# Moving the query maxima and one rounding between engines in an attention and MoE kernel

## The chip, the cores and the metric

The kernel runs on one core of a Trainium2 chip. The metric is the device time of one execution in microseconds. Five engines work side by side, each through its own list of instructions in order: TensorE (PE in the profile, its weight loads PEld), VectorE (DVE), ScalarE (ACT), GpSimd (POOL), and SyncE (SP), which issues the transfers. They wait for each other by semaphores.

## The reference

Attention with a feature map in place of the softmax, and then a two-layer network over its output. Everything is float32.

```python
def phi(x):
    proj = np.einsum('bhsd,df->bhsf', x, w_phi)
    proj = proj - np.max(np.abs(proj), axis=-1, keepdims=True)
    return np.concatenate([np.exp(proj), np.exp(-proj)], axis=-1)
q_p, k_p = (phi(q), phi(k))                     # 8 batches, 8 heads, 576 tokens, 64 -> 256
kv = np.einsum('bhsf,bhsd->bhfd', k_p, v)
z = np.sum(k_p, axis=2)
num = np.einsum('bhsf,bhfd->bhsd', q_p, kv)
den = np.einsum('bhsf,bhf->bhs', q_p, z)[..., None] + 1e-06
x = (num / den)                                 # laid out as 4608 tokens x 512
h = x @ w_in                                    # 512 -> 2048
g = np.maximum(0.01 * h, h)
out = g @ w_out                                 # 2048 -> 512
```

The maximum of the absolute projection is taken per token and head over 128 features. It is what the change is about.

## The kernel before

Two heads form an item; there are 8 batches of 4 items, 32 in all. For an item i, `k_phase(i)` makes the feature map of the keys and from it `kv` and `z`, and the query phase makes the feature map of the queries, multiplies it by them and divides. The results go into `ring`, which holds two batches of attention output. Items 0 to 7 take other forms of these phases (`first_k_phase`, `first_q_phase`, `token_q_phase`, and the `nat` branch of `k_phase`); the change does not touch them. Items 8 to 31 use `q_phase` and the other branch of `k_phase`.

Matrix products are made of float32 values that are split in two: `xh` is the value rounded to the format in which TensorE multiplies at its full rate (`F32R`), and `xl` the rest. Each product is then three: high by high, high by low, low by high. A rounding is a cast (`copy_`, line 67 on ACT, line 69 on VectorE), and the rest a subtraction (`tt_`, line 72, on POOL or VectorE). The table `ENG` says which engine does which: `"qh": "v"` puts the rounding of the query exponentials on VectorE, `"kpl": "pppv"` three of four key subtractions on POOL, and what has no entry, `"ql"` and `"gl"` among it, goes to POOL for subtractions and to ACT for copies.

`q_phase` works in a layout with features on the 128 partitions and tokens along them. For each of the two heads j and each half u of the 576 tokens, two matmuls give the projection, and a VectorE transpose of 32x32 blocks (line 380) puts it into `tq`. Line 382 takes the largest absolute value of each block row: `m` then holds, for each head, 18 values on each partition. As the transposes go block by block, the 128 features of a token are still spread over four groups of 32 partitions, and the maximum has to be taken across these groups, and given back to all four. Lines 384 to 389 do that with six small VectorE instructions: copy the upper 64 partitions next to the lower ones, take the larger of the two, the same for 32 partitions, and copy the result back to the other 32, and then to the other 64.

Then for each head, line 396 subtracts the maximum, line 398 transposes back into `mb`, and for each half lines 403 and 404 take the two exponentials on ACT into `eq`; `copy_("qh", ...)` rounds them and `tt_("ql", ...)` makes the rest. Lines 415, 416 and 418 multiply by the keys' sums, lines 420 and 421 bring numerator and denominator out of PSUM, and 424 to 429 divide. Of two buffers each are `eq` and `ql`; `qh` holds both halves of a head.

The MoE layers go by blocks of 256 tokens and 16 steps of 128 hidden features. `layer1` gives `h` in PSUM (lines 615, 616, 618); ACT makes `g` (line 622) and rounds it to `gh`, POOL subtracts to `gl`; `layer2` (lines 635 to 637) runs three steps later (`LAG`). `g`, `gh` and `gl` have two buffers each, and so has `h`. `split` rounds the attention output of the next block to `xh` and `xl`.

Nothing is ordered by hand on the engines. A scheduler places every instruction by priority, by when its inputs and buffers come free, and by durations that it assumes; attention has the better priority (`PA`) over the MoE. `advance` lets the attention run ahead, up to two batches. So what stands in an engine's list is settled before the run, and a change of engine or operation in one place moves the order everywhere behind it.

Of the kernel before, what the change touches and what calls it, by code (L numbers as in the profile page):

```python
# [9 lines left out]
F32 = mybir.dt.float32  # L10
# [4 lines left out]
ALU = mybir.AluOpType  # L15
AX = mybir.AxisListType

P = 128
# [13 lines left out]
NK = 8  # L32
BUFS = {"kph": 2, "eq": 2, "m4": 2, "g": 2, "gh": 2, "gl": 2, "ql": 2}
PBUFS = {"a": 3, "c": 1, "h": 2, "acc": 2}
ENG = {"vh": "a", "kst": "v", "qh": "v", "o": "av", "kl": "pv", "kpl": "pppv", "ksub": "vvp", "l": "v"}
TINY = 2.0 ** -15
HUGE = 2.0 ** 16 * 1.875
PF = -10 ** 6
# [6 lines left out]
def attention_moe_kernel(ctx: ExitStack, tc: tile.TileContext, q, k, v, vt, w_phi, w_in, w_out, out):  # L45
    nc = tc.nc
# [4 lines left out]
    def ct(shape, dt, name):  # L51
        return cp.tile(shape, dt, tag=name, name=name)

    def st(shape, dt, tag):
        return sp.tile(shape, dt, tag=tag, name=tag, bufs=BUFS.get(tag, 1))
# [3 lines left out]
    def pick(key):  # L59
        n = cnt[key] = cnt.get(key, -1) + 1  # L60
        e = ENG.get(key, "")
        return e[n % len(e)] if e else None

    def copy_(key, o, i):
        e = pick(key) or "a"
        if e == "a":
            nc.scalar.copy(o, i)  # L67
        else:
            (nc.vector if e == "v" else nc.gpsimd).tensor_copy(o, i)  # L69

    def tt_(key, o, a, b, op):
        (nc.vector if pick(key) == "v" else nc.gpsimd).tensor_tensor(o, a, b, op=op)  # L72

    def pt(tag):
        return ps.tile([P, 512], F32, tag=tag, name=tag, bufs=PBUFS[tag])
# [20 lines left out]
    vh = ct([P, 10, 66], F32R, "vh")  # L96
# [44 lines left out]
    for j in range(2):  # L141
        r = slice(64 * j, 64 * j + 64)
        c = slice(F * j, F * j + F)
# [39 lines left out]
    def load_q(i):  # L183
        rq = st([P, S], F32, "rq")
        nc.sync.dma_start(rq, q[i])
        qraw[i] = rq
# [112 lines left out]
    def blocks(x):  # L299
        return x.rearrange("p a b -> p (a b)").rearrange("p (c d) -> p c d", d=32)  # L300
# [60 lines left out]
    def q_phase(i):  # L361
        b, hp = divmod(i, NP)
        rq = qraw.pop(i)
        qs = st([P, 2, S], F32R, "qs")
        for j in range(2):
            o, n = slice(64 * j, 64 * j + 64), slice(64 - 64 * j, 128 - 64 * j)
            copy_("qx", qs[o, j], rq[o])
            nc.vector.tensor_tensor(qs[n, j], rq[o], qs[o, j].bitcast(F32), op=ALU.subtract)  # L368
        if i + 1 < B * NP:
            load_q(i + 1)  # L370
        yield
        tq = st([P, 2, 2, U], F32, "tq")
        m = st([P, 2, 18], F32, "m")
        for j in range(2):
            for u in range(2):
                pq = pt("a")[:, 0:U]
                rs = qs[:, j, U * u : U * u + U]
                nc.tensor.matmul(pq, lhsT=wq_h, rhs=rs, start=True, stop=False)
                nc.tensor.matmul(pq, lhsT=wq_l, rhs=rs, start=False, stop=True)
                nc.vector.transpose(tq[:, j, u], pq)  # L380
                yield
            nc.vector.tensor_reduce(m[:, j], blocks(tq[:, j]), axis=AX.X, op=ALU.max, apply_absolute_value=True)
        ms = st([64, 2, 18], F32, "ms")
        nc.vector.tensor_copy(ms, m[64:128])
        nc.vector.tensor_tensor(m[0:64], m[0:64], ms, op=ALU.max)
        nc.vector.tensor_copy(ms[0:32], m[32:64])
        nc.vector.tensor_tensor(m[0:32], m[0:32], ms[0:32], op=ALU.max)
        nc.vector.tensor_copy(m[32:64], m[0:32])
        nc.vector.tensor_copy(m[64:128], m[0:64])
        yield  # L390
        kvh, kvl = kvs_of[i]
        dn = tq[:, 0]
        qhs = st([P, 2, 2, U], F32R, "qh")
        for j in range(2):
            tj = blocks(tq[:, j])
            nc.vector.tensor_tensor(tj, tj, m[:, j].unsqueeze(2).broadcast_to([P, 18, 32]), op=ALU.subtract)  # L396
            mb = st([P, 2, U], F32, "mb")
            nc.vector.transpose(mb.rearrange("p a b -> p (a b)"), tq[:, j].rearrange("p a b -> p (a b)"))  # L398
            yield
            es = []  # L400
            for u in range(2):
                eq = st([P, 2, U], F32, "eq")
                nc.scalar.activation(eq[:, 0], mb[:, u], AF.Exp)  # L403
                nc.scalar.activation(eq[:, 1], mb[:, u], AF.Exp, scale=-1.0)  # L404
                qh = qhs[:, u]
                ql = st([P, 2, U], F32R, "ql")
                copy_("qh", qh, eq)
                tt_("ql", ql, eq, qh.bitcast(F32), ALU.subtract)
                es.append((qh, ql))
                yield  # L410
            for u in range(2):
                qh, ql = es[u]
                nm = pt("a")[:, 0:U]
                for t in range(2):
                    nc.tensor.matmul(nm, lhsT=kvh[:, j, t], rhs=qh[:, t], start=t == 0, stop=False)
                    nc.tensor.matmul(nm, lhsT=kvl[:, j, t], rhs=qh[:, t], start=False, stop=False)
                for t in range(2):
                    nc.tensor.matmul(nm, lhsT=kvh[:, j, t], rhs=ql[:, t], start=False, stop=t == 1)
                rr = slice(64 * j, 64 * j + 64)
                nc.scalar.copy(ring[rr, b % 2, hp, U * u : U * u + U], nm[0:64])  # L420
                nc.scalar.activation(dn[rr, u], nm[64:128], AF.Copy, bias=1e-6)
                yield
        dt = st([P, 2, U], F32, "mb")
        nc.vector.transpose(dt.rearrange("p a b -> p (a b)"), dn.rearrange("p a b -> p (a b)"))
        rc = st([P, 18], F32, "rc")
        nc.vector.reciprocal(rc, blocks(dt)[:, :, 0])
        nc.vector.transpose(blocks(dt), rc.unsqueeze(2).broadcast_to([P, 18, 32]))
        x = ring[:, b % 2, hp]
        tt_("x", x, x, dt.rearrange("p a b -> p (a b)"), ALU.mult)
        yield  # L430
# [153 lines left out]
    def attention():  # L584
        for i in range(NP, B * NP + 1):
            gens = [k_phase(i)] if i < B * NP else []
            if i > NP:
                gens.append((token_q_phase if i - 1 < NN else q_phase)(i - 1))
            while gens:
                for it in list(gens):  # L590
                    if next(it, end) is end:
                        gens.remove(it)
                    else:
                        yield i - 1
            yield i
# [126 lines left out]
```

## Time and profile before

| | |
|---|---|
| median of 3 runs | 1253.36 us (1252.39 to 1255.06) |
| the profiled execution | 1253.03 us, span 1251.2 us |
| PE busy | 1184.7 us, 95% of the span |
| DVE busy | 840.5 us, 67% |
| ACT busy | 804.3 us, 64% |
| POOL busy | 691.0 us, 55% |
| granted TensorE clock | 0.993 |

The span is the time from the first to the last instruction of the profiled execution; its own time is 1.8 us longer. Engines are busy while an instruction of theirs executes. Matmuls overlap in TensorE's pipeline, so that one that is listed with 284 ns may start 120 ns after the one before it. In a group's row stand line, engine, operation, output and inputs by name, shapes, count, then busy time in us and mean ns of one, then the idle time just before them and what ended it. The row of a wait says who waited for whom, us in total, times, and the longest. The first 190 us hold the loads, the weights' preparation and the first eight items; the items of the kind that the change touches follow up to about 1077 us, mixed with MoE work; the rest is MoE alone.

### The profile page before, as it was taken

To read this page: it belongs to the slowest core of one execution; us is meant where nothing else is said; L and a number is where in the kernel's file an instruction comes from. 1 tells how busy PE (TensorE), PEld (TensorE's weight loads), DVE (VectorE), ACT (ScalarE), POOL (GpSimd) and SP (SyncE) were. 2 spreads that over 40 slices of the span, in tenths; PEclk is the share of its full clock that TensorE was granted. 3 is DMA by queue.
4 is the path that set the end of the run, shared out by engine and by line. 5 is a ranking of instruction groups with operands and counts; after the bars stand their busy time and mean duration, and the time that the engine had idled before them with its cause. 6 is when DMAs were issued, how large, how long until landed. Compare 5 with 4: busy or idle time off the path is not lost. (4 is left out here: it accounts for less than half of the span.)

```text
span 1251.2 us, 21516 instructions
## 1 busy us (share of the span) xinstructions
PE 1184.7 (95%) x7654; PEld 1045.7 (84%) x7654; DVE 840.5 (67%) x1349; ACT 804.3 (64%) x2048; POOL 691.0 (55%) x724
## 2 busy tenths in 40 slices
PE   6889899999998999899999999999999999999998
PEld 5577688898887888788898888899997889999997
DVE  7999843478788877788888788854888887300000
ACT  6897865767667776666776667764776767433232
POOL 3233232457685776666676677764676867433232
PEclk9999999999998999999999999999999999999999
DMA  6544510211111101111111111020111110000000
GB/s 189 155 125 140 141 52 13 57 31 30 47 31 47 29 29 31 30 39 29 48 30 48 31 39 39 10 58 28 30 24 37 28 38 1 18 17 1 18 17 18
DMA packets 62779, 57.02 MB, mean 46 GB/s; under 512 B 45136, under 2 KB 46288, under 8 KB 62672
## 3 DMA queue, kind: packets, MB, share of 16 engines
q1 hardware_dynamic: 62672, 55.65, 15.8%
q8 instruction: 60, 0.98, 0.3%
q14 instruction: 47, 0.39, 0.1%
HBM read 46.20 MB, written 9.44 MB: 44 GB/s over the span
## 5 line engine op out<-in xcount | busy, mean ns | idle before, releaser
L72 POOL TENSOR_TENSOR gl<-g,gh 128x256 fp32r<-128x256 f32 x288 | 242.4, 846 | 275.1 <-ACT gh L67 214.7
L615 PE MATMUL h<-xh,w0h 128*128 128x256 f32 x1152 | 295.2, 284 | 6.7 <-ACT dn L567 2.2
L616 PE MATMUL h<-xh,w0l 128*128 128x256 f32 x1152 | 293.5, 282 | 1.3 <-DVE w0l L72 1.3
L615 PEld LDWEIGHTS h<-xh,w0h 128*128 128x128 f32 x1152 | 217.9, 189 | 18.7 <-ACT dn L567 3.0
L635 PE MATMUL acc<-w1h,gh 128*128 128x512 f32 x576 | 229.5, 399 | 2.9 <-DVE o L69 1.8
L636 PE MATMUL acc<-w1l,gh 128*128 128x512 f32 x576 | 228.0, 396 | 0.0
L616 PEld LDWEIGHTS h<-xh,w0l 128*128 128x128 f32 x1152 | 218.0, 189 | 11.5 <-DVE w0l L72 2.1
L637 PE MATMUL acc<-w1h,gl 128*128 128x512 f32 x576 | 218.3, 396 | 0.2 <-POOL gl L72 0.2
L618 PE MATMUL h<-xl,w0h 128*128 128x256 f32 x1152 | 201.7, 283 | 0.7 <-POOL xl L72 0.7
L622 ACT ACTIVATE g<-h 128x256 f32<-128x256 f32 x288 | 108.1, 383 | 133.0 <-PE h L618 93.1
L72 POOL TENSOR_TENSOR ql<-eq,qh 128x576 fp32r<-128x576 f32 x96 | 153.0, 1601 | 71.8 <-DVE qh L69 59.8
L618 PEld LDWEIGHTS h<-xl,w0h 128*128 128x128 f32 x1152 | 164.7, 189 | 3.1 <-POOL xl L72 2.0
L67 ACT CAST gh<-g 128x256 fp32r<-128x256 f32 x288 | 114.8, 404 | 70.4 <-PE acc L636 68.5
L72 POOL TENSOR_TENSOR kpl<-ek,kph 128x512 fp32r<-128x512 f32 x72 | 104.3, 1449 | 34.6 <-ACT kph L67 17.3
L635 PEld LDWEIGHTS acc<-w1h,gh 128*128 128x128 f32 x576 | 108.8, 189 | 16.7 <-DVE o L69 2.7
L637 PEld LDWEIGHTS acc<-w1h,gl 128*128 128x128 f32 x576 | 105.7, 188 | 19.1 <-POOL gl L72 1.3
L636 PEld LDWEIGHTS acc<-w1l,gh 128*128 128x128 f32 x576 | 109.1, 189 | 12.8
L69 DVE CAST qh<-eq 128x576 fp32r<-128x576 f32 x96 | 95.6, 1002 | 35.7 <-ACT eq L404 24.7
L250 ACT ACTIVATE ek<-pmk 128x256 f32<-128x256 f32 (+1 forms) x128 | 53.4, 417 | 64.8 <-POOL kpl L72 27.5
L69 DVE COPY o<-acc 128x512 f32<-128x512 f32 x17 | 11.5, 677 | 124.2 <-DMA out_dram<-o 124.0
L403 ACT ACTIVATE eq<-mb 128x288 f32<-128x288 f32 x96 | 42.2, 439 | 81.6 <-DVE mb L398 77.9
L72 POOL TENSOR_TENSOR ring<-ring,mb 128x576 f32<-128x576 f32 (+2 forms) x45 | 52.1, 1158 | 66.7 <-DVE mb L573 18.3
(227 smaller groups left out, 2505.6 us busy)
## 6 DMA issues: line engine op xcount, KB each, us to landing
out_dram<-o SPq DMA_DIRECT2D x35, 256.0 KB, 2.0
rk<-in_k_dram SPq DMA_DIRECT2D x30, 288.0 KB, 2.8
ring<-in_w_in_dram SPq DMA_DIRECT2D x16, 512.0 KB, 3.6
qh<-in_w_out_dram SPq DMA_DIRECT2D x16, 512.0 KB, 3.6
rq<-in_q_dram SPq DMA_DIRECT2D x28, 288.0 KB, 2.9
rv<-in_v_dram SPq DMA_DIRECT2D x30, 256.0 KB, 3.5
rv<-in_vt_dram SPq DMA_DIRECT2D x60, 32.0 KB, 2.9
f<-in_k_dram SPq DMA_DIRECT2D x2, 288.0 KB, 4.2
```

The costliest lines, as they stand in the source:

```text
L67: nc.scalar.copy(o, i)
L69: (nc.vector if e == "v" else nc.gpsimd).tensor_copy(o, i)
L72: (nc.vector if pick(key) == "v" else nc.gpsimd).tensor_tensor(o, a, b, op=op)
L250: nc.scalar.activation(ek[r, :, 0:F], pmk[r, 2 * s : 2 * s + 2], AF.Exp)
L403: nc.scalar.activation(eq[:, 0], mb[:, u], AF.Exp)
L615: nc.tensor.matmul(ph, lhsT=weight(0, "h", ft)[:, d * P : d * P + P], rhs=xh[:, d], start=d == 0, stop=False)
L616: nc.tensor.matmul(ph, lhsT=weight(0, "l", ft)[:, d * P : d * P + P], rhs=xh[:, d], start=False, stop=False)
L618: nc.tensor.matmul(ph, lhsT=weight(0, "h", ft)[:, d * P : d * P + P], rhs=xl[:, d], start=False, stop=d == NP - 1)
L622: nc.scalar.activation(g, ph, AF.Prelu, alpha=0.01)
L635: nc.tensor.matmul(a, lhsT=gh[:, ts], rhs=weight(1, "h", ft), start=ft == 0, stop=False)
L636: nc.tensor.matmul(a, lhsT=gh[:, ts], rhs=weight(1, "l", ft), start=False, stop=False)
L637: nc.tensor.matmul(a, lhsT=gl[:, ts], rhs=weight(1, "h", ft), start=False, stop=ft == NFT - 1)
```

## The change

The rounding of the query exponentials, `qh`, goes from VectorE to ACT: one letter in `ENG`. It is 96 instructions on 128x576 values.

The six small instructions become six others. `m` is now the first half of a tile `mm` of twice the size. What were copies between partition groups are now `tensor_reduce` with the maximum over a last axis of length one, which hands each value on as it is (`one`). What were two-input maxima are `tensor_reduce` over a last axis of length two: the partner's values have been put beside one's own in the other half of the tile (`mm[:, 1]`, `ms[:, 1]`), and the pair is viewed as the last axis. The values are the same.

```diff
-ENG = {"vh": "a", "kst": "v", "qh": "v", "o": "av", "kl": "pv", "kpl": "pppv", "ksub": "vvp", "l": "v"}
+ENG = {"vh": "a", "kst": "v", "qh": "a", "o": "av", "kl": "pv", "kpl": "pppv", "ksub": "vvp", "l": "v"}
...
-        m = st([P, 2, 18], F32, "m")
+        mm = st([P, 2, 2, 18], F32, "m")
+        m = mm[:, 0]
...
-        ms = st([64, 2, 18], F32, "ms")
-        nc.vector.tensor_copy(ms, m[64:128])
-        nc.vector.tensor_tensor(m[0:64], m[0:64], ms, op=ALU.max)
-        nc.vector.tensor_copy(ms[0:32], m[32:64])
-        nc.vector.tensor_tensor(m[0:32], m[0:32], ms[0:32], op=ALU.max)
-        nc.vector.tensor_copy(m[32:64], m[0:32])
-        nc.vector.tensor_copy(m[64:128], m[0:64])
+        def one(o, x):
+            nc.vector.tensor_reduce(o, x.unsqueeze(3), axis=AX.X, op=ALU.max)
+
+        ms = st([64, 2, 2, 18], F32, "ms")
+        one(mm[0:64, 1], m[64:128])
+        nc.vector.tensor_reduce(ms[0:64, 0], mm[0:64].rearrange("p s j c -> p j c s"), axis=AX.X, op=ALU.max)
+        one(ms[0:32, 1], ms[32:64, 0])
+        nc.vector.tensor_reduce(m[0:32], ms[0:32].rearrange("p s j c -> p j c s"), axis=AX.X, op=ALU.max)
+        one(m[32:64], m[0:32])
+        one(m[64:128], m[0:64])
```

The new lines shift those behind them by four: what was line 415 is 419, 635 is 639.

The order on ACT around one item's exponentials in the middle of the kernel, before. `eq` are the exponentials, numbered by buffer, `ek` and `kph` the keys' exponentials and their rounding, `pmk` the keys' projections.

```order
L403 ACTIVATE eq_6756<-mb_6749 128x288
L404 ACTIVATE eq_6756<-mb_6749 128x288
L403 ACTIVATE eq_6764<-mb_6749 128x288
L404 ACTIVATE eq_6764<-mb_6749 128x288
L622 ACTIVATE g_7106<-h_7093 128x256
L67 CAST kph_6722<-ek_6719 128x512
L67 COPY pmk_6741<-a_6742 128x256
L67 COPY pmk_6741<-a_6751 128x256
L67 CAST gh_7082<-g_7081 128x256
L403 ACTIVATE eq_6826<-mb_6822 128x288
L404 ACTIVATE eq_6826<-mb_6822 128x288
L67 CAST gh_7107<-g_7106 128x256
```

And in the changed kernel:

```order
L407 ACTIVATE eq_6756<-mb_6749 128x288
L408 ACTIVATE eq_6756<-mb_6749 128x288
L407 ACTIVATE eq_6764<-mb_6749 128x288
L408 ACTIVATE eq_6764<-mb_6749 128x288
L626 ACTIVATE g_7106<-h_7093 128x256
L67 CAST qh_6747<-eq_6756 128x576
L67 CAST qh_6747<-eq_6764 128x576
L67 CAST gh_7082<-g_7081 128x256
L250 ACTIVATE ek_6770<-pmk_6741 128x2x128
L251 ACTIVATE ek_6770<-pmk_6741 128x2x128
L407 ACTIVATE eq_6826<-mb_6822 128x288
L67 CAST kph_6773<-ek_6770 128x512
```

The first head's two casts `qh` stand behind all four of its exponentials and a `g`; `gh_7082` stands behind them, and the keys' cast and copies have moved ahead of the exponentials or behind the casts.

DVE at the small maxima of another item, before. `m` and `ms` are the maxima, `qs` the queries' rest for the next item, `kvl` the rest of the keys' sums, `o` an output block.

```order
L384 COPY ms_7195<-m_7143 64x36
L69 COPY o_7514<-acc_6886 128x512
L368 TENSOR_TENSOR qs_7603<-rq_7132,qs_7603 64x576
L385 TENSOR_TENSOR m_7143<-m_7143,ms_7195 64x36
L294 TENSOR_TENSOR kvl_6865<-c_6859,kvh_6864 128x4x64
L295 TENSOR_TENSOR kvl_6865<-c_6859,kvh_6864 128x4x64
L386 COPY ms_7195<-m_7143 32x36
L387 TENSOR_TENSOR m_7143<-m_7143,ms_7195 32x36
L388 COPY m_7143<-m_7143 32x36
L389 COPY m_7143<-m_7143 64x36
```

And in the changed kernel:

```order
L385 TENSOR_REDUCE m_7143<-m_7143 64x36
L368 TENSOR_TENSOR qs_7603<-rq_7132,qs_7603 64x576
L389 TENSOR_REDUCE ms_7195<-m_7143 64x36
L368 TENSOR_TENSOR qs_7603<-rq_7132,qs_7603 64x576
L385 TENSOR_REDUCE ms_7195<-ms_7195 32x36
L391 TENSOR_REDUCE m_7143<-ms_7195 32x36
L385 TENSOR_REDUCE m_7143<-m_7143 32x36
L385 TENSOR_REDUCE m_7143<-m_7143 64x36
```

The six have become six reductions; the subtractions for `kvl` and the output's copy, which stood between them, now stand behind.

TensorE at the first head's products of the item whose exponentials were shown, before. `a_6783` and `a_6805` are the PSUM tiles of its two halves, `h` a MoE step's.

```order
L415 MATMUL a_6783<-qh_6747,kvh_6548 128x288
L416 MATMUL a_6783<-qh_6747,kvl_6549 128x288
L415 MATMUL a_6783<-qh_6747,kvh_6548 128x288
L416 MATMUL a_6783<-qh_6747,kvl_6549 128x288
L615 MATMUL h_7378<-xh_70,w0h3_992 128x256
L616 MATMUL h_7378<-xh_70,w0l3_993 128x256
L615 MATMUL h_7378<-xh_70,w0h3_992 128x256
L616 MATMUL h_7378<-xh_70,w0l3_993 128x256
L615 MATMUL h_7378<-xh_70,w0h3_992 128x256
L616 MATMUL h_7378<-xh_70,w0l3_993 128x256
L615 MATMUL h_7378<-xh_70,w0h3_992 128x256
L616 MATMUL h_7378<-xh_70,w0l3_993 128x256
```

And in the changed kernel:

```order
L419 MATMUL a_6783<-qh_6747,kvh_6548 128x288
L420 MATMUL a_6783<-qh_6747,kvl_6549 128x288
L419 MATMUL a_6783<-qh_6747,kvh_6548 128x288
L420 MATMUL a_6783<-qh_6747,kvl_6549 128x288
L619 MATMUL h_7378<-xh_70,w0h3_992 128x256
L620 MATMUL h_7378<-xh_70,w0l3_993 128x256
L419 MATMUL a_6805<-qh_6747,kvh_6548 128x288
L420 MATMUL a_6805<-qh_6747,kvl_6549 128x288
L419 MATMUL a_6805<-qh_6747,kvh_6548 128x288
L420 MATMUL a_6805<-qh_6747,kvl_6549 128x288
L232 MATMUL a_6816<-wq_72,ks_6650 128x256 x2
```

The second half's products come after two MoE matmuls where there were eight, four of the keys' and two of the first half's own `ql` in between.

## Prediction

> **What bounds the kernel now.** I read the page's first part, then stretches of the span.
>
> ```profile
> span 1251.2 us, 21516 instructions
> ...
> PE 1184.7 (95%) x7654; PEld 1045.7 (84%) x7654; DVE 840.5 (67%) x1349; ACT 804.3 (64%) x2048; POOL 691.0 (55%) x724
> ```
>
> ```profile
> 250.00:1062.00 812.00, 777.12 (x5166) 696.17 (x5165) 647.41 (x990) 558.74 (x1458) 548.23 (x534) 1.00 0.12 33
> ...
> 500.00:562.00 62.00, 55.45 (x362) 48.63 (x362) 50.69 (x73) 41.07 (x110) 42.13 (x43) 1.00 0.13 34
> 875.00:937.00 62.00, 61.79 (x424) 56.70 (x423) 51.68 (x78) 45.83 (x117) 44.87 (x43) 1.00 0.10 25
> 1125.00:1187.00 62.00, 62.00 (x400) 56.25 (x399) 0.69 (x1) 19.04 (x49) 18.63 (x27) 1.00 0.03 10
> ```
>
> The first three columns after the bounds are the stretch's length, TensorE and its weight loads, then DVE, ACT and POOL. TensorE is busy 95% of the span, so it sets the end. In the last row, where only the MoE layers are left, it has no gap. From 250 to 1062 us, where the 24 head pairs of the form that the change touches run (one each 812/24 = 33.8 us), it is idle 812 - 777.1 = 34.9 us. Everything that a change on DVE or ACT can give is in that idle time, since what the change touches first runs at 261.7 us (a row below). The next view is that of TensorE's waits there, its ten longest rows.
>
> ```profile
> PE c L212 <- DVE kvl L295: 5.4, 7, 1.6
> PE c L212 <- POOL kpl L72: 3.8, 5, 1.9
> PE a L415 <- DVE qh L69: 3.6, 7, 0.7
> PE a L378 <- DVE tq L380: 3.1, 5, 1.1
> PE a L415 <- DVE pmk L237: 2.8, 7, 0.6
> PE a L415 <- ACT tq L421: 1.9, 3, 0.9
> PE a L418 <- POOL ql L72: 1.8, 3, 0.8
> PE acc L635 <- DVE o L69: 1.8, 2, 1.3
> PE h L615 <- ACT xh L67: 1.7, 3, 1.0
> PE a L378 <- DVE pmk L237: 1.7, 4, 0.9
> ```
>
> DVE ended 5.4 + 3.6 + 3.1 + 2.8 + 1.8 + 1.7 = 18.4 us of them, POOL 5.6, ACT 3.6: 27.6 us in 46 waits. A wait costs more than the idle time that it shows, since the matmul before it is still counted:
>
> ```profile
> 508.10 0.28 PE L616 MATMUL h<-xh,w0l 128*128 128x256 f32 x1
> 508.22 0.28 PE L615 MATMUL h<-xh,w0h 128*128 128x256 f32 x1
> ...
> 510.17 0.31 PE L212 MATMUL c<-kph,vh 128*66 128x256 f32 x1 [0.83 <-DVE kvl L295]
> ```
>
> Matmuls of 0.28 us start 0.12 us apart when nothing holds them, so the last 0.16 us of each overlap the next. At a stall they overlap nothing: 46 x 0.16 = 7.4 us. With them, these waits are worth 35 us, which is the ceiling.
>
> Why is DVE late? Not for want of time on average (647 of 812 us), but because single instructions take far longer than their size says.
>
> ```profile
> L386 DVE COPY ms<-m x24: 170/328/1312, 269.3 to 1063.3; 32x36 f32<-32x36 f32 x24
> ```
>
> Durations here are least, median and most: the same copy of 36 values takes 0.17 us or 1.3 us. The timelines of DVE and of POOL for the same microseconds show when:
>
> ```profile
> 505.51 1.25 DVE L386 COPY ms<-m 32x36 f32<-32x36 f32 x1
> ```
>
> ```profile
> 505.45 1.29 POOL L72 TENSOR_TENSOR kpl<-ek,kph 128x512 fp32r<-128x512 f32 x1 [1.52 <-ACT kph L67]
> ```
>
> The copy began 0.06 us after POOL's subtraction and ended as that ended. The two engines exclude each other. Instructions with one input and no copying form do not show it: the reductions of the same stage keep to a narrow band although POOL is busy 548 of 812 us, and so do ACT's instructions.
>
> ```profile
> L382 DVE TENSOR_REDUCE m<-tq x48: 705/753/755, 261.7 to 1062.0; 128x18 f32<-128x576 f32 x48
> ```
>
> ```profile
> L250 ACT ACTIVATE ek<-pmk x128: 400/417/442, 82.0 to 1054.8; 128x256 f32<-128x256 f32 x104, 64x256 f32<-64x256 f32 x24
> ```
>
> [...]
>
> **The change part by part.** Taken off DVE: 96 casts, and 24 times six small instructions.
>
> ```profile
> L69 DVE CAST qh<-eq 128x576 fp32r<-128x576 f32 x96 | 95.6, 1002 | 35.7 <-ACT eq L404 24.7 <-POOL ql L72 4.4 <-POOL gl L72 3.8
> ...
> L386 DVE COPY ms<-m 32x36 f32<-32x36 f32 x24 | 12.1, 503 | 0.8
> ...
> L387 DVE TENSOR_TENSOR m<-m,ms 32x36 f32<-32x36 f32 x24 | 11.2, 466 | 0.8
> L385 DVE TENSOR_TENSOR m<-m,ms 64x36 f32<-64x36 f32 x24 | 11.1, 461 | 0.7
> ...
> L388 DVE COPY m<-m 32x36 f32<-32x36 f32 x24 | 9.3, 387 | 0.8
> ...
> L384 DVE COPY ms<-m 64x36 f32<-64x36 f32 x24 | 8.6, 359 | 0.6
> ...
> L389 DVE COPY m<-m 64x36 f32<-64x36 f32 x24 | 7.3, 304 | 0.8
> ```
>
> The casts are 95.6 us. The six are 503 + 466 + 461 + 387 + 359 + 304 = 2480 ns an item, 59.5 us in all.
>
> Put on DVE: six reductions an item, four of 36 values and two of 72.
>
> ```profile
> L382 DVE TENSOR_REDUCE m<-tq 128x18 f32<-128x576 f32 x48 | 35.6, 743 | 1.1
> ...
> L240 DVE TENSOR_REDUCE m<-pmk 64x2 f32<-64x256 f32 x24 | 10.0, 417 | 0.8
> ```
>
> No row has a reduction as small. From 417 ns at 256 values to 743 at 576 is 1.02 ns a value and 156 ns fixed, so 193 and 229 ns: 4 x 193 + 2 x 229 = 1230 ns, 29.5 us in all. Lower bound: the 170 ns that the copies reach, 24.5 us. Upper bound: 417 ns each, 60 us, which would leave that half without a gain. I take 29.5, on the line of the rows. DVE is thus freed of 95.6 + 59.5 - 29.5 = 125.6 us, 5.2 us an item. It was busy 647/24 = 27.0 of 33.8 us, so its idle time goes from 6.8 to 12.0 us.
>
> Put on ACT: 96 casts of 128x576.
>
> ```profile
> L67 ACT CAST qs<-rq 64x576 fp32r<-64x576 f32 x48 | 32.3, 673 | 4.1 <-PE a L379 3.4
> ...
> L67 ACT CAST kph<-ek 128x512 fp32r<-128x512 f32 x96 | 59.3, 617 | 0.9
> ...
> L67 ACT CAST vh<-rv 128x640 fp32r<-128x640 f32 x24 | 17.5, 731 | 0.3 <-DMA rv<-in_vt_dram 0.2
> ```
>
> The length per partition sets ACT's time (617 ns at 512, 673 at 576, 731 at 640), so 673 ns: 64.6 us, between 617 and 731 ns each 59 to 70. ACT in the stage goes from 558.7 to 623 of 812 us, its idle time from 253 to 189 us. The row of ACT's exponentials above (400 to 442 ns) shows no lock, so I look for no long ones. [...] The trace's casts take 441 ns at best and 990 in the median, so the measurement speaks for the exchange.
>
> How the data moves: before, the first half's cast ran on DVE while ACT did the second half's exponentials; POOL's subtraction `ql` waits for the cast.
>
> ```profile
> L415 PE MATMUL a<-qh,kvh x192: 288/295/408, 277.1 to 1076.9; 128*128 128x288 f32 x192
> ...
> L69 DVE CAST qh<-eq x96: 441/990/1700, 275.1 to 1073.2; 128x576 fp32r<-128x576 f32 x96
> L72 POOL TENSOR_TENSOR ql<-eq,qh x96: 1402/1442/1999, 276.0 to 1074.9; 128x576 fp32r<-128x576 f32 x96
> ```
>
> Now the cast stands in ACT's own queue behind up to two more exponentials, and the second half's work starts 0.67 us later for it. In exchange the cast no longer waits for POOL: 0.67 us for 0.99 in the median. I price the chain at nothing; the cover is POOL's `ql` of the first half, 1.44 us, for which the second half's has to wait anyway and under which a cast fits. Without that cover each half would be 0.67 us later, 48 x 0.67 = 32 us of lateness, which TensorE would feel as far as it has no MoE matmul to do. What is queued behind the casts on ACT is the MoE's `g` and `gh`, for which POOL's `gl` and then TensorE wait.
>
> The sum for TensorE. The 3.6 us on DVE's `qh` go. The other 14.8 us behind DVE shrink as its idle time grows, by 6.8/12.0, to 8.4: 6.4 less. Of some 21 copies, casts and two-input instructions that DVE has for an item, 4 + 6 are removed, so half of POOL's own hold-ups should go (`ql` takes 1.44 us in the median and up to 2.00); I take a third off its 5.6 us, 1.9. With the 0.16 us that belong to each wait (7.4 x 11.9/27.6 = 3.2), 15.1 us are gained. Against that, ACT's 3.6 us grow by 253/189 to 4.8, and I let half of the `qh` wait come back under ACT's name, 1.8; with overlap 3.5 us. Net 11.6 us. Bounds: 35 us if all these waits go; a loss is the first rival's. Start and end are untouched: the last attention matmul starts at 1076.9 us and 174 us of MoE follow. The span of 1251.2 becomes 1239.6; the profiled execution had 1253.03, 1.8 more, and lies 0.3 under the median of the three runs, so **1241 us**.
>
> **Rivals.** *ACT becomes the bound.* ACT works in order and already waits often:
>
> ```profile
> ACT gh L67 <- PE acc L636: 68.5, 90, 3.4
> ```
>
> (The numbers are us in total, times, and the longest.) With two buffers each, `g` and `gh` have little lead; a cast in front of them delays TensorE's next layer. The place is `g`/`gh` behind `qh`; each cast is 0.67 us. If 15.1/64.6 = 23% of the casts' time reaches TensorE the gain is gone; at 40% the time is 1253 - 15.1 + 25.8 = 1264. For it: ACT's list is 77% full then and comes in bursts. Against it: TensorE's waits on ACT are 3.6 of 27.6 us now, at 69%.
>
> *The waits only move.* The whole order is rebuilt, and a full DVE alone makes no stall: from 875 to 937 us it is busy 83% of the time and TensorE idle 0.2 us, while from 500 to 562, with 82%, TensorE loses 6.5. If it matters more where the order puts matmuls, other waits take the place of these: 1253, give or take 2.5. Against it: the stall at 510.17 us stands behind a DVE queue in which one copy alone, that at 505.51, was held up by 1.08 us.
>
> *The maxima gain nothing.* If the reductions cost 417 ns or meet the lock after all, DVE is freed of 95 us instead of 126, 4.0 us an item: 6.8/10.8 leaves 9.3 of the 14.8, about 1 us less gain, 1242. That is inside the likeliest's own range.
>
> *Nearly all stalls go*, POOL's too, because removing half of the exclusions lets DVE and POOL both keep up: three quarters of 35 us, 26 us, 1227.
>
> **How the numbers follow.** The likeliest, with the small maxima case, has 0.55 and its own range 1232 to 1249; nearly all stalls gone 0.07; moved waits 0.17; ACT as the bound 0.21. What a measurement can tell from no change is 0.2%, 2.5 us. Faster 0.62, same 0.17, slower 0.21. The range of 1228 to 1262 leaves out the best of the fast case and the worst of the slow one.
>
> **What would show it.** Right: reductions of 0.17 to 0.25 us with no long ones; `qh` casts on ACT at 0.67 us; DVE near 715 us and ACT near 869 in the page's first part; `ql` and `gl` with a lower mean; TensorE's waits on DVE in the stage under 11 us and its idle time there near 24. Wrong: rows of TensorE waiting for ACT `g`, `gh` or `qh` over 10 us, or a stage whose idle time is as before under other names.

## The result

The changed kernel takes 1218.47 us in the median of four runs (1216.81 to 1220.53), the kernel before 1252.88 beside it: 0.9723 of it, with a 95% interval of 0.9704 to 0.9743, or 34.4 us less. 1241 was forecast, and the range ended at 1228. The sign was right and the size was wrong by a factor of three.

The first part of the page after, and the stretches of its span (length, TensorE, weight loads, DVE, ACT, POOL, granted clock):

```profile
span 1218.8 us, 21505 instructions
...
PE 1169.9 (96%) x7654; PEld 1046.7 (86%) x7654; DVE 715.2 (59%) x1253; ACT 859.0 (70%) x2144; POOL 672.5 (55%) x724
```

```profile
0.00:250.00 250.00, 220.45 (x1311) 180.17 (x1312) 179.71 (x334) 181.54 (x422) 78.11 (x105) 0.98 0.38 108
250.00:1062.00 812.00, 796.87 (x5384) 729.19 (x5383) 532.70 (x915) 629.52 (x1596) 545.57 (x550) 0.99 0.13 34
...
500.00:562.00 62.00, 61.23 (x422) 56.50 (x421) 41.45 (x68) 50.65 (x129) 43.49 (x47) 1.00 0.12 33
875.00:937.00 62.00, 62.00 (x429) 57.40 (x428) 42.20 (x75) 50.42 (x128) 43.14 (x45) 1.00 0.14 39
```

And the first stretch of the kernel before, which the prediction did not show:

```profile
0.00:250.00 250.00, 222.72 (x1321) 182.80 (x1322) 179.19 (x334) 182.62 (x425) 79.22 (x106) 0.98 0.39 109
```

DVE has lost 125.3 us of busy time (840.5 to 715.2; 125.6 were expected) and ACT has gained 54.7 (64.6 expected). The first 250 us are as they were, 1311 matmuls against 1321. The gain lies from 250 to 1062 us, as expected, and there the number of matmuls tells more than the idle time. TensorE is idle 15.1 us instead of 34.9, which is 19.8 less, but it starts 5384 matmuls instead of 5166 in the same 812 us. 218 in 5384 is 4.0%, or 33 us of the 812, which is the whole gain; the busy time of the weight loads grew by the same 33.0 us (696.2 to 729.2). So 13 us of it came from gaps that the idle time never showed.

TensorE's waits in the stretch of the prediction's list (us in total, times, longest), the ten longest. That list goes from 188 to 1062 us, not from 250 as the prediction has it; 0.5 us of its 27.6 lies ahead of 250.

```profile
PE c L212 <- POOL kpl L72: 2.1, 3, 0.7
PE acc L641 <- POOL rv L180: 1.8, 1, 1.8
PE h L619 <- ACT g L626: 1.5, 3, 0.8
PE a L419 <- ACT tq L425: 1.5, 1, 1.5
PE c L212 <- ACT kph L67: 1.4, 5, 0.7
PE h L619 <- ACT xh L67: 1.3, 2, 0.8
PE a L232 <- ACT tq L425: 1.3, 1, 1.3
PE c L212 <- DVE kph L270: 1.1, 1, 1.1
PE acc L639 <- DVE o L69: 1.0, 3, 0.4
PE a L419 <- ACT qh L67: 0.8, 2, 0.6
```

Of the six rows of DVE that made 18.4 us only the output's copy is left, with 1.0 in place of 1.8, and one of 1.1 for `kph` is new; `kvl`, `tq` and `pmk` are no longer among the ten. ACT's six rows make 7.8 us.

The instructions that were exchanged (least, median and most ns of one):

```profile
L389 DVE TENSOR_REDUCE ms<-m x24: 211/222/226, 269.8 to 1038.3; 64x36 f32<-64x72 f32 x24
L385 DVE TENSOR_REDUCE ms<-ms x24: 177/178/179, 270.0 to 1038.6; 32x36 f32<-32x36 f32 x24
L391 DVE TENSOR_REDUCE m<-ms x24: 208/218/224, 270.3 to 1038.8; 32x36 f32<-32x72 f32 x24
```

```profile
L67 ACT CAST qh<-eq x96: 657/667/697, 275.8 to 1050.4; 128x576 fp32r<-128x576 f32 x96
L72 POOL TENSOR_TENSOR ql<-eq,qh x96: 1412/1442/2006, 276.7 to 1052.8; 128x576 fp32r<-128x576 f32 x96
```

The reductions take 0.18 and 0.22 us and none is long; the casts take 0.67 us on ACT and none is long. Both are as the prediction had them. POOL's `ql` is as uneven as it was.

### The profile page after: what moved, and what is told of

Its sections match the earlier page's. It is cut to its first block, busy times and chain, and to the rows that moved or that the text cites. A ratio compares the mean times of both kernels' runs of the same rounds, so it can differ in the third digit from the quotient of the medians.

```text
span 1218.8 us, 21505 instructions
## 1 busy us (share of the span) xinstructions
PE 1169.9 (96%) x7654; PEld 1046.7 (86%) x7654; DVE 715.2 (59%) x1253; ACT 859.0 (70%) x2144; POOL 672.5 (55%) x724
## 3 DMA queue, kind: packets, MB, share of 16 engines
q1 hardware_dynamic: 62672, 55.65, 16.3%
## 4 chain that ended last, share of the span: by engine, by line
PE 71%; DVE 13%; ACT 9%; issue 4%; DMA 2%; POOL 1%; SPq 1%; ACTq 0%; DVEq 0%; POOLq 0%
PE h L619 9%; PE h L620 9%; PE h L622 9%; PE acc L641 9%; PE acc L639 9%; PE acc L640 9%; PE c L212 6%; PE a L232 2%; PE a L419 2%; PE a L422 2%; PE a L420 2%; PE a L333 1%; DVE ql L162 1%; DVE ql L165 1%; DMA ring<-in_w_in_dram 1%
## 5 line engine op out<-in xcount | busy, mean ns | idle before, releaser
L72 POOL TENSOR_TENSOR gl<-g,gh 128x256 fp32r<-128x256 f32 x288 | 237.0, 827 | 280.1 <-ACT gh L67 225.7
L72 POOL TENSOR_TENSOR ql<-eq,qh 128x576 fp32r<-128x576 f32 x96 | 151.0, 1591 | 19.8 <-ACT qh L67 13.2
L72 POOL TENSOR_TENSOR kpl<-ek,kph 128x512 fp32r<-128x512 f32 x72 | 96.5, 1341 | 74.5 <-ACT kph L67 39.6
L639 PEld LDWEIGHTS acc<-w1h,gh 128*128 128x128 f32 x576 | 109.0, 189 | 15.6 <-DVE o L69 2.3
L202 DVE TENSOR_TENSOR ks<-rk,ks 64x576 fp32r<-64x576 f32 x48 | 63.0, 1313 | 99.9 <-ACT ks L67 99.1
L250 ACT ACTIVATE ek<-pmk 128x256 f32<-128x256 f32 (+1 forms) x128 | 53.3, 417 | 34.8 <-POOL kpl L72 18.4
L72 POOL TENSOR_TENSOR xl<-ring,xh 128x256 fp32r<-128x256 f32 (+3 forms) x96 | 59.1, 643 | 9.4 <-ACT xh L67 7.5
```

Of the source, the lines that this page charges most:

```text
L202: nc.vector.tensor_tensor(ks[n, j], rk[o], ks[o, j].bitcast(F32), op=ALU.subtract)
L250: nc.scalar.activation(ek[r, :, 0:F], pmk[r, 2 * s : 2 * s + 2], AF.Exp)
L639: nc.tensor.matmul(a, lhsT=gh[:, ts], rhs=weight(1, "h", ft), start=ft == 0, stop=False)
```

## The experiments

Two theories stood against each other first. By the one (A), what is saved is the time in which DVE and POOL hold each other up; by the other (B), it is DVE's time as such. A third (C) was that the scheduler's new order happens to be a better one. All kernels were run beside the kernel before.

**Each half alone.** The casts on ACT with the maxima as before, and the new maxima with the casts on DVE:

```diff
# casts_alone, from the kernel before
-ENG = {... "qh": "v", ...}
+ENG = {... "qh": "a", ...}
# maxima_alone, from the changed kernel
-ENG = {... "qh": "a", ...}
+ENG = {... "qh": "v", ...}
```

> Before with the 96 qh casts on ACT, the six small maxima as they were. Theory A (exclusion: what is saved is the time that DVE and POOL hold each other up): the casts' surplus over 0.46 us is 52 us of DVE, that of the six over 0.18 us is 34 us, so of the 34 us gained 21 come here: 1232. Theory B (load: what counts is DVE time as such): 95.6 of the 125.6 us freed, so 26 us: 1227. Theory C (a lucky order): no proportion, anything from 1218 to 1255.

> The six reductions as in the change, the qh casts left on DVE. Theory A: 34 of 86 us of surplus, 13 us gained: 1240. Theory B: 30 of 125.6 us, 8 us gained: 1245. Theory C: no proportion. If the two parts add, this gain and that of casts_alone make 34 us.

Measured: 1227.30 us for the casts (0.9795 of before, 0.978 to 0.9811) and 1218.76 for the maxima (0.9728, 0.9711 to 0.9746). They do not add: 25 and 34 us against 34 for both. In this order the maxima have the whole gain, with little DVE time freed. The stretch from 250 to 1062 us of maxima_alone, the busy time of its engines over the whole run, and its cast:

```profile
250.00:1062.00 812.00, 795.40 (x5377) 727.23 (x5377) 634.46 (x1011) 573.56 (x1497) 572.53 (x548) 0.99 0.12 34
```

```profile
PE 1169.7 (96%) x7654; PEld 1047.1 (86%) x7654; DVE 817.6 (67%) x1349; ACT 804.1 (66%) x2048; POOL 701.1 (58%) x724
```

```profile
L69 DVE CAST qh<-eq x96: 447/900/1698, 273.4 to 1038.9; 128x576 fp32r<-128x576 f32 x96
```

Over the run DVE is busy 817.6 us, 22.9 fewer than before, where the change freed 125.3; TensorE starts 5377 matmuls in the stretch all the same. Theory B had the casts' time (1227), but 1245 for the maxima, so DVE's busy time is a bad measure of what a change is worth; theory A, with 1232 and 1240, missed both, the maxima by 21 us. Parts that do not add pointed to C.

**The order.** Three rewrites leave the work of the change alone and move other work; each was made on both kernels. The first two leave each engine as much to do as it had; the third gives POOL more (busy 702.0 us in place of 691.0 in the kernel before):

```diff
# before_rotated, after_rotated: the third of four key subtractions to DVE, not the fourth
-"kpl": "pppv"
+"kpl": "ppvp"
# before_o_swapped, after_o_swapped: output copies on DVE and ACT by turns, the other way round
-"o": "av"
+"o": "va"
# before_ksub_moved, after_ksub_moved: POOL subtracts the maximum of the keys' second group, not of the third
-"ksub": "vvp"
+"ksub": "vpv"
```

> The kernel before with the same work in another order: of four key subtractions the third instead of the fourth goes to DVE. Theory C (the result hangs on the order) expects a time 5 us or more away from 1253; theories A and B expect 1248 to 1258.

> The changed kernel with the same rotation of the key subtractions. Theories A and B expect 1214 to 1224, so that the distance to before_rotated stays at 34 us give or take 6. Theory C expects the distance to be another, under 20 or over 45 us.

> Before with the copies of the output blocks swapped between ACT and DVE (first block on DVE, second on ACT, in place of the other way): nothing that the change touches, and the same amount of work on each engine, but another order behind it. Theory D (the order of before is a bad one by chance, and the change alone is worth about the 16 us between the rotated pair): 1220 to 1240. Theory E (the stalls come with the place of the fourth key subtraction and with the exclusions, whatever the rest of the order): 1249 to 1257.

> The changed kernel with the same swap. Theory D: 1208 to 1222, and 10 to 20 us faster than before_o_swapped. Theory E: 1214 to 1222, about 34 us faster than before_o_swapped.

> Before with the one of three keys' subtractions of the maximum that goes to POOL moved from the third group of an item to the second (twice as large, so 24 x 0.7 us more for POOL and less for DVE). Another order, the maxima, casts and the fourth key subtraction as in before. Theory D: 1220 to 1245. Theory E: 1245 to 1257.

> The changed kernel with the keys' subtraction of the maximum on POOL moved from the third group to the second, as in before_ksub_moved (1244.0). The pairs so far are 34.4, 15.6 and 31.6 us apart. If the change is worth 27 us and the order is chance of some 10: 1207 to 1227.

The other order is worth as much as the change (us, median of four runs each, the kernel before 1252 to 1253 beside them):

| order | before | changed | difference |
|---|---|---|---|
| as it was | 1252.88 | 1218.47 | 34.4 |
| key subtractions rotated | 1225.09 | 1209.45 | 15.6 |
| output copies swapped | 1235.77 | 1204.20 | 31.6 |
| maximum's subtraction moved | 1244.03 | 1223.38 | 20.7 |
| mean | 1239.4 | 1213.9 | 25.6 |

Theories A and B missed both rotated kernels (1248 to 1258 and 1214 to 1224), and the distance of 15.6 is as C had it. The kernel before is the slowest of its four orders, and the change is faster than its partner in every one of them. The mean difference is 25.6 us, with a standard error of 4.4 from the four (their spread of 8.9 by the root of four). With so few orders a 95% interval reaches some 14 us to either side. So 25.6 us is the best estimate of the part that belongs to the change, and by it the other 9 us of the 34 belong to this pair of orders. Theory E, as the expectations call it, failed clearly for before_o_swapped (1235.8 where it had 1249 or more) and by 1 us for before_ksub_moved. Theory D had both these times, but not that of after_o_swapped (1204.2 where it had 1208 or more, and E 1214 or more), nor the distance of that pair, 31.6 us where it had 10 to 20. The longest waits of TensorE in the rotated kernel before (188 to 1062 us):

```profile
PE a L415 <- DVE qh L69: 8.5, 10, 2.7
PE a L232 <- DVE ks L202: 3.8, 5, 1.4
PE h L615 <- ACT xh L67: 2.0, 2, 1.5
```

The two longest rows of before, 5.4 us for `kvl` and 3.8 for POOL's `kpl`, have gone, although `kvl` is made as before and POOL has as many `kpl` to do; those for `qh` and `ks` have grown (from 3.6 and 0.5 us). The order decides which late result TensorE meets.

**The halves in three orders.**

> maxima_alone with the key subtractions rotated. Over three orders before has a mean of 1237.8 us and the change 1210.7, 27.1 apart. If exclusion sets the shares (surplus of the six 34 us, of the casts 52 us), the maxima alone are worth 11 us in the mean over the orders, 1227, with some 10 us of chance in one order: 1217 to 1237 here. If they are worth all of it, as maxima_alone says (1218.8), the mean is 1211 and this one 1203 to 1219.

> maxima_alone with the output copies swapped. As for maxima_rotated: 1217 to 1237 if exclusion sets the shares, 1203 to 1219 if the maxima are worth all of it.

> casts_alone with the key subtractions rotated. If exclusion sets the shares the casts are worth 16 us in the mean over three orders, 1222, and 1212 to 1232 here. If ACT takes back what DVE gains, the mean is 1232 or more, as before rotated.

> casts_alone with the output copies swapped. As for casts_rotated: 1212 to 1232 if exclusion sets the shares, a mean of 1232 or more if ACT takes back the gain.

| | as it was | rotated | o swapped | mean | from before |
|---|---|---|---|---|---|
| before | 1252.88 | 1225.09 | 1235.77 | 1237.9 | |
| casts alone | 1227.30 | 1227.87 | 1224.92 | 1226.7 | 11.2 |
| maxima alone | 1218.76 | 1213.10 | 1223.28 | 1218.4 | 19.5 |
| both | 1218.47 | 1209.45 | 1204.20 | 1210.7 | 27.2 |

In the means the halves add within the chance of the order: 11.2 (standard error 8.2) and 19.5 (7.3) make 30.7, and 27.2 were measured. The surplus of time had said 16 us for the casts and 11 for the maxima. The single runs do not decide it: maxima_rotated lies where the maxima are worth all, maxima_o_swapped where exclusion sets the shares, and both runs of the casts where exclusion had them. Against each other, the maxima alone (59.5 us of DVE before, 27.8 after) are faster than the casts alone (95.6 us) in every order, by 8.5, 14.8 and 1.6 us. That is 8.3 in the mean with a standard error of 3.8, which three orders do not make certain. Shares by freed DVE time, which would put the casts 14 us ahead, lie nearly six standard errors from it. In a single order each half can look like anything: rotated, the casts alone are 2.8 us slower than nothing.

**Exclusion by itself.** Six instructions on 36 values were added behind the maxima of each item, into a scratch half that nobody reads, once as copies and once as reductions:

```diff
         one(m[64:128], m[0:64])
+        for _ in range(6):
+            nc.vector.tensor_copy(ms[:, 0], m[64:128])     # six_copies_added
+            one(ms[:, 0], m[64:128])                        # six_reduces_added
```

> The change, and behind the six reductions of each of the 24 items six copies of 36 values into a scratch half of ms (nobody reads it). Unhindered they are 6 x 0.17 = 1.0 us an item, 25 us of DVE in all. Theory A (exclusion): some four in ten begin while POOL works and take 0.75 us, so about 59 us of DVE, and POOL is held up too: 5 to 13 us slower, 1224 to 1231. Theory B (load): at 34 us gained per 125.6 us of DVE, and the same time for copies as for reductions, 7 us: 1225, the same as with reductions added.

> The change, and behind the six reductions of each item six more reductions of 36 values into the scratch half, in place of the copies of six_copies_added. 6 x 0.19 us an item, 27 us of DVE. Theory A: no exclusion, 0 to 3 us: 1218 to 1221, and clearly faster than six_copies_added. Theory B: 27/125.6 of 34 us, 7 us: 1225, the same as six_copies_added.

Measured: 1231.66 us with the copies (13.2 more than the change) and 1221.85 with the reductions (3.4 more), each less than 1 us above what theory A had at the most. The rows of the added instructions (least, median, most), of the copies and then of the reductions, 144 of each:

```profile
L395 DVE COPY ms<-m x144: 177/180/1361, 269.8 to 1057.7; 64x36 f32<-64x36 f32 x144
```

```profile
L385 DVE TENSOR_REDUCE ms<-m x144: 177/185/189, 270.5 to 1049.5; 64x36 f32<-64x36 f32 x144
```

The same number of values to the same place takes 0.18 us in both forms at the least, and up to 1.36 us as a copy, never over 0.19 as a reduction. One long copy, and what POOL did meanwhile:

```profile
509.11 1.25 DVE L395 COPY ms<-m 64x36 f32<-64x36 f32 x1
```

```profile
509.04 1.29 POOL L72 TENSOR_TENSOR kpl<-ek,kph 128x512 fp32r<-128x512 f32 x1 [0.21 <-PE c L212]
```

The start and end times of the traces say the same of all of them. Of the 144 copies, 73 began while a subtraction of POOL ran and took 640 ns in the median; the other 71 took 181 ns at the most. Of the 144 reductions, 75 began under such a subtraction, and these too took 189 ns at the most. So DVE waits for POOL in the one form and not in the other. The 9.8 us between the two times agree with it, but they are one pair in one order, and orders alone have made more.

**The cast without the exclusion.** The rounding as a maximum over one value, on DVE:

```diff
-                copy_("qh", qh, eq)
+                nc.vector.tensor_reduce(qh, eq.unsqueeze(3), axis=AX.X, op=ALU.max)
```

> The change, but the rounding qh is a maximum over an axis of length one on DVE (a reduction that writes the rounded format), in place of the cast on ACT. DVE keeps 96 x 0.75 = 72 us of it, more than an unhindered cast of 0.46 us would take. Theory A: nothing is excluded, so most of the gain stays: 1218 to 1226. Theory B: only 54 of the 125.6 us are freed, 15 us gained: 1238, and ACT is spared 64 us. Theory C: no proportion.

> cast_as_reduce (1203 us) with the key subtractions rotated as in after_rotated, in the hope of a kernel that beats both. If the two gains are independent, 1203 - 9 = 1194; if both only take away the same stalls, 1200 to 1204; if the order is a matter of chance, anything from 1195 to 1212.

> cast_as_reduce with the output copies swapped. The reduction has 1203.3 and 1206.8 in two orders, the change 1218.5, 1209.5 and 1204.2 in three. If sparing ACT its 64 us is worth something, this is at or under 1204 and the mean at least 5 us under the change's 1210.7; if not, it is 1207 to 1217.

```profile
L411 DVE TENSOR_REDUCE qh<-eq x96: 727/752/756, 273.6 to 1029.5; 128x576 fp32r<-128x576 f32 x96
```

```profile
250.00:1062.00 812.00, 803.77 (x5481) 740.75 (x5480) 601.10 (x1011) 581.75 (x1515) 560.59 (x562) 1.00 0.12 34
```

The rounding takes 0.75 us every time, more than an unhindered cast and less than the mean of the casts (1.00). The kernel takes 1203.29 us (0.9604 of before, 0.9589 to 0.9619), the fastest of this study and 15 us faster than the change, with DVE busier by 68 us in the stretch; theory A (1218 or more) and theory B (1238) had it slower. In the other two orders it takes 1206.75 and 1211.89; the mean of 1207.3 is 3.4 us under that of the change, which the chance of the order covers. So the reduction on DVE is as good a place for the rounding as ACT, as far as three orders can tell, and whether it is a better one stays open. The hope that reduction and rotation add did not come true.

**ACT's time.** Every cast done twice:

```diff
                 copy_("qh", qh, eq)
+                copy_("qh", qh, eq)
```

> The change with every qh cast done twice on ACT, one after the other (same values): 64 us more of ACT and 0.67 us more of latency for each half. If ACT time is nearly free, as the profile of the changed kernel suggests (TensorE waits 7 us on ACT in all), at most 4 us are lost: 1218 to 1222. If ACT is close to being the bound, a quarter of the 64 us or more is lost: 1234 or over.

Measured: 1250.24 us (0.9982 of before, 0.9972 to 0.9991), 31.8 us more than the change. That is half of the 64 us that ACT does more, so the second cast was not nearly free. It is one order only, and the cast also makes each half 0.67 us later; the run does not tell ACT's load from this delay. Two stretches of this kernel, around 380 and 540 us (length, TensorE, weight loads, DVE, ACT, POOL, clock), and TensorE's longest waits from 370 to 560 us:

```profile
374.00:388.00 14.00, 7.10 (x30) 6.04 (x31) 6.96 (x17) 10.08 (x24) 5.31 (x4) 0.52 0.10 35
...
520.00:531.00 11.00, 9.06 (x56) 7.69 (x54) 3.54 (x3) 10.05 (x24) 9.62 (x12) 1.00 0.00 1
531.00:552.00 21.00, 13.95 (x59) 12.48 (x60) 15.53 (x29) 13.25 (x32) 9.17 (x9) 0.52 0.24 69
552.00:562.00 10.00, 10.00 (x72) 9.38 (x71) 5.62 (x10) 7.87 (x21) 5.48 (x7) 0.99 0.01 2
```

```profile
PE c L212 <- ACT kph L67: 11.8, 5, 5.7
PE a L420 <- ACT qh L67: 2.4, 1, 2.4
```

```profile
383.07 0.48 PE L212 MATMUL c<-kph,vh 128*66 128x256 f32 x1 [5.66 <-ACT kph L67]
```

```profile
533.46 0.48 PE L212 MATMUL c<-kph,vh 128*66 128x256 f32 x1 [2.94 <-ACT kph L67]
```

TensorE waits for `kph` on ACT, 5.7 us at the longest. Near these waits its clock is granted at half, for most of 14 us and of 21 us. The first of the two had begun at about 375 us, ahead of the wait of 5.7 us, so that wait did not set it off. Over the span the mean clock is 0.971, against 0.988 for the change: 1.7% of 1249 us is 21 us, which is an estimate of what the clock takes of the 31.8 us at the most, since waits and slow matmuls overlap.

## Why the prediction was wrong

**TensorE sets the end, and the gain lies between 250 and 1062 us.** Right; the first 250 us gained nothing, and the last stage runs at the rate that it had (398 matmuls from 1125 to 1187 us, 400 before).

**The sum of 11.6 us.** This is the step that failed. By the prediction's terms TensorE's idle time falls by 3.6 + 6.4 + 1.9 - 3.0 = 8.9 us, and the overlap that goes with the waits adds 2.7. Measured were 19.8 us of idle time and 13 us behind it: both terms were too small, by 10.9 and 10.5 us. (The 3.0 us on ACT's side with their overlap are 3.8 by the prediction's own rate, not 3.5; this changes nothing.)

**The ceiling of 35 us.** Not passed, but wrongly made: 33 us were gained, and 15.1 us of idle time are left. Its terms were the idle time of the ten longest rows and 0.16 us for each of their 46 waits. A gap shorter than the 0.16 us by which a matmul outlasts the start of the next shows as no idle time at all, and the smaller rows were left out. The prediction's own rows had a better measure: from 875 to 937 us the kernel before started 424 matmuls, 6.84 a microsecond; at that rate the 812 us would have held 5553 and not 5166, and 387 of 6.84 a microsecond are 57 us, an estimate, as even that stretch was not quite full. The change got 33 us of these.

**DVE and POOL exclude each other (the prediction's "lock") in the copies, the casts and the two-input maxima, not in the reductions.** Right, and shown by the added copies and reductions. Of the casts of `qh` before, 26 began with no subtraction of POOL running and took 461 ns at the most, the other 70 took 1010 in the median; of the 48 two-input maxima, 29 began so and took 190 ns at the most, the other 19 took 734 in the median. Durations were right to a few per cent: 180 and 219 ns for the reductions (193 and 229 were forecast), 671 ns in the mean for the casts on ACT:

```profile
L67 ACT CAST qh<-eq 128x576 fp32r<-128x576 f32 x96 | 62.5, 671 | 0.2
...
L389 DVE TENSOR_REDUCE ms<-m 64x36 f32<-64x72 f32 x24 | 5.3, 220 | 0.5
L391 DVE TENSOR_REDUCE m<-ms 32x36 f32<-32x72 f32 x24 | 5.2, 218 | 0.8
```

**TensorE's waits on DVE shrink with DVE's idle time, 18.4 to 8.4 us.** Wrong in size, and most of the first shortfall: with the 3.6 us on `qh`, 10.0 us were to go, and the ten longest rows have lost 16.3, from 18.4 to 2.1. Busy time was the wrong measure, as maxima_alone shows with 22.9 us of DVE freed and nearly all the matmuls of the change.

**The maxima as the smaller part, priced with the casts by the microsecond.** Wrong. By the prediction, maxima that free nothing would have cost 1 us of the gain. In the means of three orders the maxima are worth 19.5 us and the casts 11.2, though which is worth more is not certain. The six stand one behind another between the projections and all exponentials of an item, and what one of them is held up the item is late; the casts are two by two, with other work between. In the traces the time from an item's last row maximum (line 382, then 383) to its first subtraction (line 396, then 400) is 4.91 us in the mean before and 4.93 with the casts alone, but 3.58 with the maxima alone and with both. That this is the reason was not tested by itself, and it is not the only one: the rotated kernel before has 4.96 us there and is 28 us faster. The doubled casts suggest why the casts gain less than they free: what DVE gets back, ACT has to do, and that has a price.

**POOL is held up half as often, a third of its waits go.** The size was right, 1.7 us where 1.9 were taken off: POOL's rows among the ten are 3.9 us in place of 5.6, with 1.8 of them for a memset of `rv` that had no row before. The mechanism is shown only in part. POOL's busy time fell from 691.0 to 672.5 us, but the means of `ql` and `gl` hardly did (1601 to 1591 ns and 846 to 827), and `ql` has the same median and the same longest.

**ACT costs 3.5 us.** For the change itself its rows grew from 3.6 to 7.8 us, as forecast in kind. The rival that ACT becomes the bound did not come true at this dose, but at twice the dose, in one order, half of the added time reached TensorE, well over the 23% that was put down as the point where the gain is gone.

**The rivals.** "Nearly all stalls go", 1227 with a chance of 0.07, came nearest in the number; of its stalls those behind DVE went, those behind POOL mostly stayed. "The maxima gain nothing" was wrong: no reduction was long. "The waits only move" was wrong as an outcome and right as a mechanism: the order of before alone, by rewrites that take no work away, was worth 9 to 28 us. No step of the prediction held a term for that, and the range had none. Against the mean over four orders, 25.6 us, the forecast of 11.6 is less than half, and lies at the edge of what four orders leave possible; the rest of the 34.4, some 9 us, is put down to the order, and is luck. What share of the 25.6 us comes from the exclusion itself stays open: only the added copies and reductions tested it alone, in one order.

## What to carry to other kernels

Where a scheduler rebuilds the whole list, one pair of times measures the change and the luck of two orders; rewrite something unrelated in both kernels and compare means before a gain or a loss of 1 to 2% is believed. Read a stall's cost from matmuls started per microsecond against a stretch that is never starved, and not from idle time, which hides every gap shorter than the pipeline's overlap, 0.16 us here for matmuls of 128x256. Look at least and longest of one instruction's durations: the copy of 36 values that takes 0.17 or 1.3 us was waiting for the other engine. Where such instructions follow one another, a form of the same operation that does not take part, here a maximum over one value, can be worth more than the engine time that it saves suggests: the maxima freed 31.7 us of DVE and the casts 95.6, and the maxima were worth no less.

## What was not expected of the hardware

TensorE's clock was granted at half for 6.8 us after a stretch in which no idle gap was longer than 1.64 us. In the kernel before:

```profile
372.00:386.40 14.40, 9.97 (x54) 7.11 (x52) 13.25 (x17) 10.11 (x26) 11.12 (x9) 1.00 0.13 47
386.40:393.20 6.80, 6.03 (x25) 5.20 (x25) 5.19 (x10) 3.42 (x9) 4.25 (x4) 0.50 0.16 43
393.20:400.00 6.80, 6.71 (x51) 6.26 (x51) 6.53 (x11) 5.25 (x12) 1.83 (x3) 1.00 0.01 2
```

In 14.4 us TensorE was busy 10.0, and for the next 6.8 us it was granted half its clock. The longest of the gaps, in brackets:

```profile
374.88 0.31 PE L212 MATMUL c<-kph,vh 128*66 128x256 f32 x1 [1.64 <-DVE kvl L295]
...
383.53 0.53 PE L418 MATMUL a<-ql,kvh 128*128 128x288 f32 x2 [0.73 <-POOL ql L72]
384.85 0.40 PE L415 MATMUL a<-qh,kvh 128*128 128x288 f32 x1 [0.79 <-ACT tq L421]
```

With the casts doubled the mean clock was 0.52 in two stretches, of 14 and of 21 us. What sets it to half was not tested by any run here.

And a `tensor_reduce` over an axis of length one can write TensorE's rounded format in the place of a cast, at 0.727 to 0.756 us for 576 values a partition, while POOL was busy 560.6 of 812 us. In the kernel before, matmuls of 128x256 on values in that format started 0.12 us apart (line 618, median), those on plain float32 0.22 us (line 333).
